# Three-pass products summed in one PSUM bank, with the difference product scaled in place

## The chip, the cores and the metric

The kernel runs on one core of a Trainium2 chip. The metric is the device time of one execution in microseconds, as the median of several runs. A separate profiled execution gives the instruction trace from which all durations below are read. TensorE (PE) does the matrix products, VectorE (DVE), ScalarE (ACT) and GpSimd (POOL) work element by element, and SyncE (SP) issues most transfers.

## The reference

Two blocks follow each other. The first is a polynomial attention over 4 batches, 4 heads, 1088 tokens and a head size of 32: queries and keys are sketched to 64 features, and attention is linear in them. Its output becomes a matrix x of 4352 tokens by 128 columns. The second block is a gated feed-forward layer, and the change lies in it:

```python
g = x @ w_gate                      # 4352x128 @ 128x1536
silu = g * (1.0 / (1.0 + np.exp(-g)))
val = x @ w_val                     # 128x1536
return (silu * val @ w_out)         # 1536x128
```

## The kernel before

**Layout.** Everything is kept transposed: xT has 128 columns of x on the partitions and tokens along the free axis. The tokens are cut into blocks, three small ones of batch 0 first (`HEAD`), and then seven from batch 1 on, six of 480 tokens and a last one of 384 (`line`). The 1536 hidden columns are cut into 12 chunks of 128. A **unit** is one block with one chunk: a gate product g, a value product, Silu of g, and their product, which is the hidden piece hj in one of the `slots`. A **down** product multiplies a hidden piece with its chunk of w_out and sums 12 of them in one PSUM bank; `store` transposes the sum and sends it out. Where line[3:6] meets the chunks in `FINE`, the down product is itself made in three passes from a cut hidden piece (`cut_hidden`: ScalarE cuts, GpSimd takes the rest, VectorE makes the difference).

**Three-pass products.** TensorE makes a plain float32 product in two slow passes. In the loop that the change touches, most products are made instead from rounded pieces in a faster number format (called cut products below). A matrix w is cut into a high part w1, and a rest w0 which is scaled up to wb = BETA * w0; x is cut into x1 and x0; wd and xd are differences, wd = w1 - wb and xd = x1 - BETA * x0, with BETA = 4096. Then

w x = (1 + 1/BETA) * (w1 x1 + wb x0) - (1/BETA) * wd xd,

apart from rounding. That takes three passes in place of two that each last about twice as long.

**The loop.** The loop at L1353 goes through 84 units y = 0 to 83 (`END`), each with `i, j = line[y // 12], y % 12`. For y below 20 (`GATES`) the value product alone has three passes, and the gate product is plain (L977); from 20 on both have three (`both`). One unit (`cut_unit`, L966) is: the difference products wd xd (L975) into one bank or a pair; ScalarE scales them by -1/BETA into an SBUF buffer `sums` (L979); TensorE makes w1 x1 and wb x0 in another bank or pair (L985, L986); VectorE scales that by 1 + 1/BETA and adds `sums` (L987); ScalarE takes Silu (L993); GpSimd multiplies Silu with the value sum into hj (L998). With both, the last two are put off to the next unit (`ending`, `finish`). The very last unit, y = 83, is a plain one of two float32 products (`unit`, L1361, L1022).

After each unit come the down products of units that lie five or more back (L1366), and pieces of other work that are woven in: steps of the attention of later batches (`parts_of`, `group`), cutting of tokens (`cut_tokens`), of gate weights (`gate_rows`) and of down weights (`down_steps`). The lists `before` and `behind` hold work of cut hidden pieces that is due at a given unit.

**PSUM.** PS is eight banks of 512 float32 columns. `used` notes when each was last handed out, `held` those that may not be. `bank` gives the one that was used longest ago (from the loop on), `pair` the pair out of (0,1), (4,5), (6,7) that was, `wide` a named pair ("a" is 4,5 and "b" is 6,7). Bank 3 ("acc") is kept for down sums, bank 2 ("g2") too from unit 20 on. The handing out only chooses; what makes engines wait is the scheduler's tracking of who still reads or writes a bank.

**Groups.** At y = 4, 6, 20, 22 and 40 a group of TensorE work of the attention is put ahead of the unit: key sums and key sketches (y = 4), query sketches (6), numerators of batch 2 and key sums of batch 3 (20), query sketches (22), numerators of batch 3 (40). `numerators` (L767) makes small products into two pairs of banks, alternating between both pairs (L777), and then ScalarE copies the first pair to xT and VectorE the second (L794). `sketched` (L576) uses one pair, from which ScalarE copies.

**The end.** After the loop, 12 products of 128 columns (L1095, `straight`) with the roles of the operands exchanged make the last 128 tokens, with the rest of the down products of the last block between them; then a copy (L1384) and the last transfers (L1390).

Of the kernel before, what the change touches and what calls it, by code (L numbers as in the profile page):

```python
# [7 lines left out]
FP32 = mybir.dt.float32  # L8
# [11 lines left out]
def kernel(  # L20
# [28 lines left out]
    nc = tc.nc  # L49
# [48 lines left out]
    def touch(*which):  # L98
        for i in which:
            clock[0] += 1  # L100
            used[i] = clock[0]

    def hold(*tags):
        for t in tags:
            held.update((place[t], place[t] + 1) if t in "ab" else (place[t],))

    def release(*tags):
        for t in tags:
            banks = (place[t], place[t] + 1) if t in "ab" else (place[t],)
            held.difference_update(banks)  # L110
            touch(*banks)
# [10 lines left out]
        touch(i)  # L122
        return PS[:, i, :]

    def pair():

        i = min((i for i in (0, 4, 6) if i not in held), key=lambda i: max(used[i], used[i + 1]))
        touch(i, i + 1)
        return PS[:, i : i + 2, :]

    def wide(tag):
        i = place[tag]
# [475 lines left out]
    def attentions():  # L608

        yield from turn_keys(1)
        yield from turn_queries(1)
        hold("a")
        kp = wide("a")
        for i, c in enumerate(kpieces):
            key_products(kp[:, i, :], *c)
        ka = apool.tile([P, NC * H, R], FP32, tag="kas", name="kas")

        def sketch(ps, i):  # L620
            c0, c1 = kpieces[i]
            return ps[:, i, 0 : 64 * (c1 - c0)].rearrange("p (x t r) -> p x t r", t=2, r=R)

        for i, (c0, c1) in enumerate(kpieces):
            nc.scalar.copy(ka[:, H * c0 : H * c1, :], sketch(kp, i)[:, :, 0, :])
        phk = apool.tile([P, NC, H, R, R], FP32, tag="phk", name="phk")
        for n, (i, c0, c1) in enumerate(((0, 0, 3), (0, 3, 5), (1, 5, 7), (1, 7, 9))):
            first = H * (c0 - kpieces[i][0])
            kb = sketch(kp, i)[:, first : first + H * (c1 - c0), 1, :]
            key_features(phk, (ka[:, H * c0 : H * c1, :], kb), c0, c1)  # L630
            if n == 3:
                release("a")
            if n % 3 != 1:
                yield
        zs, sums = feature_sums(phk)
        for f in sums:
            f()
        yield from turn_keys(2)
        kvz = wide("a")
        key_values(kvz[:, 0, 0:F], phk, 0, NC)  # L640
        value_sums(kvz[:, 0, :], zs)
        kab, kcopies = sketched(wide("b"), key_products, 2, "kab2")
        fold(kvz[:, 0, :])
        spread = spread_out(1, kvz[:, 0, :])
        hold("a", "b")
        yield
        qab, copies = sketched(wide("a"), query_sketches, 3, "qab")
        run_copies(copies, 2)
        yield
        run_copies(kcopies, 2)  # L650
        release("a", "b")
        for n, _ in enumerate(query_step(1, qab)):
            if n % 2 == 1:
                yield
        yield
        yield
        numerators(1, spread)
        yield "first"

        phk = apool.tile([P, NC, H, R, R], FP32, tag="phk", name="phk")  # L660
        yield from features(phk, kab)
        zs, sums = feature_sums(phk)
        for f in sums:
            f()
        yield from turn_keys(3)
        yield from turn_queries(2)
        for b in (2, 3):
            yield "pe"
            if b == 3:
                numerators(2, spread)  # L670
            hold("a")
            kv = bank()
            kv_bank = [max(used, key=used.get)]
            release("a")
            key_values(kv[:, 0:F], phk, 0, NC)
            if b == 2:
                kab, copies = sketched(wide("a"), key_products, 2, "kab2")
                run_copies(copies, 2)
            value_sums(kv, zs)
            fold(kv)  # L680
            spread = spread_out(b, kv)
            touch(*kv_bank)
            yield
            yield "pe"
            qab, copies = sketched(wide("b"), query_sketches, 3, "qab")
            run_copies(copies, 2)
            yield
            if b == 2:
                yield from turn_queries(3)
                phk = late[:, NL - 6 :, :].rearrange("p s (n h i j) -> p (s n) h i j", h=1, i=R, j=R)  # L690
                phk = phk.rearrange("p (c h) o i j -> p c (h o) i j", h=H)
                yield from features(phk, kab)
                zs, sums = feature_sums(phk)
            yield from beside(query_step(b, qab), sums)
        yield "pe"
        numerators(3, spread)
        yield

# [65 lines left out]
            )  # L764
            yield

    def numerators(b, spread):  # L767
        kvr = spread[:].rearrange("p h (g d) -> p h g d", g=2)
        phT = turned[b]
        num = wide("a"), wide("b")  # L770
        for g in range(2):
            for s in range(H):
                for a in range(4):
# [162 lines left out]
    def cut_hidden(y, i, j):  # L936

        if not h_sets:
            x = []
            for tag in ("kld", "qld", "vld", "kT", "qT"):  # L940
                t = const.tile([P, 2, WB], F32R, tag=tag, name="h" + tag, bufs=1)
                x += [t[:, k, :] for k in range(2)]
            h_sets.extend(x[k : k + 3] for k in range(0, 9, 3))
        n = blocks[i][1]
        h_sets.append(h_sets.pop(0))
        h1, h0, hd = h_parts[i, j] = [x[:, 0:n] for x in h_sets[-1]]
        h = hidden[i, j][:, 0:n]
        add_to(behind, y + 2, lambda: nc.scalar.activation(h1, h, AF.Copy, scale=CUT))
        add_to(before, y + 3, lambda: nc.gpsimd.tensor_tensor(
            out=h0, in0=h, in1=whole(h1), op=ALU.subtract  # L950
        ))
        add_to(before, y + 4, lambda: nc.vector.scalar_tensor_tensor(
            out=hd, in0=whole(h0), scalar=-BETA, in1=whole(h1), op0=ALU.mult, op1=ALU.add
        ))

# [7 lines left out]
        room[1] += k  # L963
        return room[0][:, at : at + k, :]

    def cut_unit(i, j, both=False, y=None):  # L966

        t0, n = blocks[i]
        x1, x0, xd = (x[:, 0:n] for x in x_parts[i])
        ws = (wg, wv) if both else (wv,)  # L970
        parts = [[x[:, j % 3, :] for x in w_parts[id(w), j // 3]] for w in ws]
        ds = pair()[:, :, 0:n] if both else bank()[:, 0:n].unsqueeze(1)
        g = None if both else bank()[:, 0:n]
        for k, (_, _, wd) in enumerate(parts):
            nc.tensor.matmul(ds[:, k], wd, xd, start=True, stop=True)  # L975
        if not both:
            nc.tensor.matmul(g, wg[:, j, :], xT[:, t0 : t0 + n], start=True, stop=True)  # L977
        sums = doubles(len(ws))[:, :, 0:n]
        nc.scalar.activation(sums, ds, AF.Copy, scale=-1.0 / BETA)  # L979
        now(before, y)  # L980
        finish()
        now(behind, y)
        ps = pair()[:, :, 0:n] if both else bank()[:, 0:n].unsqueeze(1)
        for k, (w1, wb, _) in enumerate(parts):
            nc.tensor.matmul(ps[:, k], w1, x1, start=True, stop=False)  # L985
            nc.tensor.matmul(ps[:, k], wb, x0, start=False, stop=True)  # L986
        nc.vector.scalar_tensor_tensor(  # L987
            out=sums, in0=ps, scalar=1.0 + 1.0 / BETA, in1=sums, op0=ALU.mult, op1=ALU.add
        )

        def last():
            sg = fpool.tile([P, WB], FP32, tag="sg", name="sg", bufs=5)[:, 0:n]
            nc.scalar.activation(sg, sums[:, 0] if both else g, AF.Silu)  # L993
            slot_of[i, j] = slots.pop(0)
            hj = slot_of[i, j]
            hidden[i, j] = hj
            todo.append((i, j))
            nc.gpsimd.tensor_tensor(out=hj[:, 0:n], in0=sg, in1=sums[:, len(ws) - 1], op=ALU.mult)  # L998
            if (i, j) in DOWN:
                cut_hidden(y, i, j)  # L1000

        if both:
            ending.append(last)
        else:
            last()


    ending = []

    def finish():  # L1010
        while ending:
            ending.pop(0)()

    def unit(i, j, late=False, between=(None, None)):

# [334 lines left out]
    lows = [late[:, c, :].rearrange("p (c f) -> p c f", f=P) for c in range(4)]  # L1350
    gate_rows = []
    down_steps = cut_down()
    for y in range(END):  # L1353
        i, j = line[y // NCH], y % NCH
        if y in GROUPS:
            group()
        if y == GATES:
            hold("g2")
        if y == END - 1:
            finish()  # L1360
            unit(i, j)  # L1361
        else:
            cut_unit(i, j, both=y >= GATES, y=y)
        for _ in range(2):

            if len(todo) > min(5 + (todo[0] == (line[1], 0)), END - y + 1):  # L1366
# [54 lines left out]
```

## Time and profile before

| what | value |
|---|---|
| median of 3 runs | 284.03 us (283.66 to 284.04) |
| the profiled execution's own time | 283.83 us |
| its span (first to last instruction) | 282.0 us |
| TensorE clock granted | 0.999 of full |
| loop over units, from the first L975 to the last L1022 | about 92.4 to 273.6 us |
| VectorE's scale-and-add L987, 83 of them | 83.1 us busy, 1003 ns mean |
| ScalarE's scaling L979, 83 | 70.9 us busy, 854 ns mean |

In the rows of the profile, "PE" is a product and "PEld" its weight load, which runs beside the product before it. A product's row covers its way through the array too, so rows overlap: a 480-column cut product's row is 0.38 us long, though the next product starts 0.22 us after it. "out<-in" names the tiles, with 128x480 for 128 partitions and 480 columns. After the bar stand busy time, mean length of one, and the engine's idle time just before with what ended it. In the chain of waits, each piece is followed back from the last instruction to what released it; its time is that between releases, not the row's length. A granted clock of 1.0 means that TensorE was not slowed.

### The profile page before, as it was taken

The page shows a single profiled execution, that of the slowest core. Times are in us where ns is not written, and L with a number is a line of the kernel's source. Part 1 is how long each engine was busy: PE and PEld are TensorE (multiplying, and loading weights), DVE is VectorE, ACT ScalarE, POOL GpSimd, SP SyncE. Part 2 cuts the span into 40 slices and gives each one's busy share as a digit, 9 for nine tenths or more (in the row PEclk, how much of TensorE's full clock was granted, in tenths as well). Part 3 has the DMA queues.
Part 4 walks back from the last instruction along what each step waited for, and adds up shares of the span by engine and source line. Part 5 has one row for each costly group of instructions (what it writes and reads, how often), then busy time and mean ns, then how long its engine had stood idle before and what let it go on. Part 6 is the DMA issues. An engine that isn't in the chain of part 4 may idle for free.

```text
span 282.0 us, 5606 instructions
## 1 busy us (share of the span) xinstructions
PE 275.8 (98%) x2132; PEld 191.7 (68%) x2132; DVE 226.1 (80%) x327; ACT 177.2 (63%) x322; POOL 181.8 (64%) x176
## 2 busy tenths in 40 slices
PE   8899999999999999999999999999999999999994
PEld 7545565666656676555576776757787777778984
DVE  3997987976495977999668899749999999999741
ACT  3468666633401756645368787768888898887850
POOL 3314432279510797489935887759989999898660
PEclk9999999999999999999999999999999999999999
DMA  6574194222231123000100020001000200010021
GB/s 194 160 223 106 41 278 154 81 79 79 59 68 28 27 90 86 2 0 10 29 16 0 1 35 2 0 2 29 6 0 1 37 0 1 9 29 0 2 33 30
DMA packets 26139, 14.30 MB, mean 51 GB/s; under 512 B 19840, under 2 KB 24192, under 8 KB 26112
## 3 DMA queue, kind: packets, MB, share of 16 engines
q1 hardware_dynamic: 25456, 13.84, 19.3%
q8 instruction: 17, 0.28, 0.4%
q10 hardware_dynamic: 656, 0.10, 0.2%
q14 instruction: 10, 0.08, 0.1%
HBM read 11.41 MB, written 2.23 MB: 48 GB/s over the span
## 4 chain that ended last, share of the span: by engine, by line
PE 94%; DVE 2%; DMA 2%; ACT 1%; issue 0%; SPq 0%
PE PS L1067 26%; PE PS L1022 16%; PE PS L975 11%; PE PS L985 11%; PE PS L986 11%; PE PS L977 6%; PE PS L777 2%; PE PS L347 2%; PE PS L335 2%; PE PS L381 2%; DMA kld<-in_k_dram 2%; PE PS L1062 1%; PE PS L1059 1%; PE PS L1061 1%; PE PS L1095 1%; PE PS L490 1%
## 5 line engine op out<-in xcount | busy, mean ns | idle before, releaser
L998 POOL TENSOR_TENSOR hbuf<-sg,sum 128x480 f32<-128x480 f32 (+1 forms) x83 | 105.1, 1271 | 30.5 <-ACT sg L993 24.0
L987 DVE SCALAR_TENSOR_TENSOR sum<-PS,sum 128x960 f32<-128x960 f32 (+2 forms) x83 | 83.1, 1003 | 18.8 <-ACT sum L979 13.8
L979 ACT ACTIVATE sum<-PS 128x960 f32<-128x960 f32 (+2 forms) x83 | 70.9, 854 | 35.1 <-PE PS L975 34.2
L1067 PE MATMUL PS<-hbuf,wo 128*128 128x480 f32 (+3 forms) x142 | 57.5, 505 | 0.0
L975 PE MATMUL PS<-xd,gphq 128*128 128x480 f32 (+1 forms) x63 | 38.8, 616 | 0.0
L985 PE MATMUL PS<-x,w 128*128 128x480 f32 (+1 forms) x83 | 38.5, 464 | 0.0
L993 ACT ACTIVATE sg<-sum 128x480 f32<-128x480 f32 (+1 forms) x63 | 36.7, 582 | 1.6 <-DVE sum L987 1.3
L975 PE MATMUL PS<-xd,wd 128*128 128x480 f32 (+1 forms) x83 | 36.0, 433 | 0.0
L1067 PEld LDWEIGHTS PS<-hbuf,wo 128*128 128x128 f32 x142 | 26.6, 189 | 8.4 <-issue 0.9
L986 PE MATMUL PS<-x,wb 128*128 128x480 f32 (+1 forms) x83 | 31.2, 376 | 0.0
L1022 PE MATMUL PS<-xT,wg 128*128 128x384 f32 (+1 forms) x74 | 29.5, 480 | 0.0
L1022 PE MATMUL PS<-xT,wv 128*128 128x384 f32 (+1 forms) x74 | 28.8, 471 | 0.2 <-DVE wv L279 0.2
L1026 ACT ACTIVATE sg<-PS 128x384 f32<-128x384 f32 (+1 forms) x31 | 14.3, 466 | 21.4 <-PE PS L1022 19.6
L985 PE MATMUL PS<-x,graw 128*128 128x480 f32 (+1 forms) x63 | 23.5, 373 | 0.2 <-ACT xT L794 0.2
L975 PEld LDWEIGHTS PS<-xd,wd 128*128 128x128 f32 x83 | 15.7, 189 | 11.5 <-issue 10.0
L986 PE MATMUL PS<-x,graw 128*128 128x480 f32 (+1 forms) x63 | 23.3, 370 | 0.0
L1067 PE MATMUL PS<-hbuf,scaled 128*128 128x480 f32 x42 | 20.3, 564 | 0.0
L1022 PEld LDWEIGHTS PS<-xT,wv 128*128 128x128 f32 x74 | 13.8, 190 | 9.2 <-DVE hbuf L1037 0.9
L1022 PEld LDWEIGHTS PS<-xT,wg 128*128 128x128 f32 x74 | 13.3, 189 | 9.3 <-issue 1.2
L985 PEld LDWEIGHTS PS<-x,w 128*128 128x128 f32 x83 | 15.6, 188 | 5.8 <-issue 3.4
L986 PEld LDWEIGHTS PS<-x,wb 128*128 128x128 f32 x83 | 15.6, 188 | 5.7 <-issue 4.3
L977 PE MATMUL PS<-xT,wg 128*128 128x480 f32 x40 | 19.3, 564 | 0.0
(173 smaller groups left out, 466.5 us busy)
## 6 DMA issues: line engine op xcount, KB each, us to landing
kld<-in_k_dram SPq DMA_DIRECT2D x4, 544.0 KB, 4.2
vld<-in_v_dram SPq DMA_DIRECT2D x12, 144.0 KB, 4.5
qld<-in_q_dram SPq DMA_DIRECT2D x3, 544.0 KB, 3.4
raw<-in_moe_w_out_dram SPq DMA_DIRECT2D x4, 384.0 KB, 4.0
raw<-in_moe_w_gate_dram SPq DMA_DIRECT2D x3, 384.0 KB, 3.5
raw<-in_moe_w_val_dram SPq DMA_DIRECT2D x3, 384.0 KB, 3.8
out_dram<-o SPq DMA_DIRECT2D x16, 60.0 KB, 1.9
vld<-in_v_dram SPq DMA_DIRECT2D x4, 112.0 KB, 4.2
```

The lines of the kernel that those rows point to most:

```text
L335: nc.tensor.matmul(ps[32 * a : 32 * a + 32, 96 * (c - c0) : 96 * (c - c0) + 96], qT[:, 4 * c + a, :], s123[:, a : a + H, :, :].rearrange(" ...
L975: nc.tensor.matmul(ds[:, k], wd, xd, start=True, stop=True)
L977: nc.tensor.matmul(g, wg[:, j, :], xT[:, t0 : t0 + n], start=True, stop=True)
L979: nc.scalar.activation(sums, ds, AF.Copy, scale=-1.0 / BETA)
L985: nc.tensor.matmul(ps[:, k], w1, x1, start=True, stop=False)
L986: nc.tensor.matmul(ps[:, k], wb, x0, start=False, stop=True)
L987: nc.vector.scalar_tensor_tensor(out=sums, in0=ps, scalar=1.0 + 1.0 / BETA, in1=sums, op0=ALU.mult, op1=ALU.add)
L993: nc.scalar.activation(sg, sums[:, 0] if both else g, AF.Silu)
L998: nc.gpsimd.tensor_tensor(out=hj[:, 0:n], in0=sg, in1=sums[:, len(ws) - 1], op=ALU.mult)
L1022: nc.tensor.matmul(o[:, 0:n], w[:, j, :], xT[:, t0 : t0 + n], start=True, stop=True)
L1026: nc.scalar.activation(sg[:, 0:n], g[:, 0:n], AF.Silu)
L1067: nc.tensor.matmul(acc[i][:, 0:n], w, hidden[i, j][:, 0:n], **sides)
```

## The change

A unit is split into `start_unit` and `finish_unit`, and the loop starts unit y + 1 before it finishes unit y. All of a unit happens in one pair of banks, which is held from the start until the end: bank 0 of the pair is for the gate, bank 1 for the value. `start_unit` makes the difference product(s) there, and ScalarE scales them in place, by -1/(BETA * WHOLE) with WHOLE = 1 + 1/BETA. `finish_unit` lets TensorE add w1 x1 and wb x0 onto the scaled difference (`start=False`; for y below 20 a plain gate product goes into bank 0). Silu then reads PSUM, with WHOLE as its scale, and VectorE multiplies the value sum in PSUM by WHOLE and by Silu straight into hj. The buffer `sums`, VectorE's scale-and-add and GpSimd's product are gone, as are `ending` and `finish`. Every unit, the last too, is made so. `cut_hidden`'s steps are due one unit sooner. `pair` can hold the pair that it gives, and `let_go` frees it. In the loop the attention takes pairs by `pair()` in place of the named ones, and the key sums take bank 2; the numerators of batch 1, ahead of the loop, keep the named pairs.

```diff
-    def pair():
+    def pair(keep=None):
         i = min((i for i in (0, 4, 6) if i not in held), key=lambda i: max(used[i], used[i + 1]))
         touch(i, i + 1)
+        if keep is not None:
+            held.add(i)
+            kept[keep] = i
         return PS[:, i : i + 2, :]
+    kept = {}
+    def let_go(keep):
+        i = kept.pop(keep)
+        held.discard(i)
+        touch(i, i + 1)
...
-        numerators(1, spread)
+        numerators(1, spread, (wide("a"), wide("b")))
...
-            hold("a")
-            kv = bank()
-            kv_bank = [max(used, key=used.get)]
-            release("a")
+            kv = bank("g2")
...
-                kab, copies = sketched(wide("a"), key_products, 2, "kab2")
+                kab, copies = sketched(pair(), key_products, 2, "kab2")
...
-            qab, copies = sketched(wide("b"), query_sketches, 3, "qab")
+            qab, copies = sketched(pair(), query_sketches, 3, "qab")
...
-        num = wide("a"), wide("b")
+        num = num or (pair(), pair())
...
-        add_to(behind, y + 2, lambda: nc.scalar.activation(h1, h, AF.Copy, scale=CUT))
-        add_to(before, y + 3, lambda: nc.gpsimd.tensor_tensor(
+        add_to(behind, y + 1, lambda: nc.scalar.activation(h1, h, AF.Copy, scale=CUT))
+        add_to(before, y + 2, lambda: nc.gpsimd.tensor_tensor(
...
-        add_to(before, y + 4, lambda: nc.vector.scalar_tensor_tensor(
+        add_to(before, y + 3, lambda: nc.vector.scalar_tensor_tensor(
...
+    WHOLE = 1.0 + 1.0 / BETA
+    sums_of = {}
+    def start_unit(y, both=False):
+        i, j = line[y // NCH], y % NCH
+        n = blocks[i][1]
+        xd = x_parts[i][2][:, 0:n]
+        ws = (wg, wv) if both else (wv,)
+        ps = sums_of[y] = pair(y)[:, :, 0:n]
+        for w in ws:
+            nc.tensor.matmul(
+                ps[:, w is wv], w_parts[id(w), j // 3][2][:, j % 3, :], xd, start=True, stop=True
+            )
+        d = ps if both else ps[:, 1]
+        nc.scalar.activation(d, d, AF.Copy, scale=-1.0 / BETA / WHOLE)
+    def finish_unit(y, both=False):
+        i, j = line[y // NCH], y % NCH
+        t0, n = blocks[i]
+        x1, x0, _ = (x[:, 0:n] for x in x_parts[i])
+        ps = sums_of.pop(y)
+        now(before, y)
+        for w in (wg, wv):
+            if w is wg and not both:
+                nc.tensor.matmul(
+                    ps[:, 0], wg[:, j, :], xT[:, t0 : t0 + n], start=True, stop=True
+                )
+                continue
+            w1, wb = (w_parts[id(w), j // 3][k][:, j % 3, :] for k in range(2))
+            nc.tensor.matmul(ps[:, w is wv], w1, x1, start=False, stop=False, skip_group_check=True)
+            nc.tensor.matmul(ps[:, w is wv], wb, x0, start=False, stop=True, skip_group_check=True)
+        sg = fpool.tile([P, WB], FP32, tag="sg", name="sg", bufs=5)[:, 0:n]
+        nc.scalar.activation(sg, ps[:, 0], AF.Silu, scale=WHOLE if both else 1.0)
...
+        nc.vector.scalar_tensor_tensor(
+            out=hj[:, 0:n], in0=ps[:, 1], scalar=WHOLE, in1=sg, op0=ALU.mult, op1=ALU.mult
+        )
+        let_go(y)
+        now(behind, y)
+        if (i, j) in DOWN:
+            cut_hidden(y, i, j)
...
+    start_unit(0)
     for y in range(END):
...
-        if y == END - 1:
-            finish()
-            unit(i, j)
-        else:
-            cut_unit(i, j, both=y >= GATES, y=y)
+        if y + 1 < END:
+            start_unit(y + 1, y + 1 >= GATES)
+        finish_unit(y, y >= GATES)
```

More of the change, by code (lines that the diff above doesn't have):

```diff
@@ L681, in attentions @@
             spread = spread_out(b, kv)
-            touch(*kv_bank)
             yield
             yield "pe"
-            qab, copies = sketched(wide("b"), query_sketches, 3, "qab")
+            qab, copies = sketched(pair(), query_sketches, 3, "qab")
             run_copies(copies, 2)
@@ L765, in query_step, with numerators @@
             yield
-    def numerators(b, spread):
+    def numerators(b, spread, num=None):
         kvr = spread[:].rearrange("p h (g d) -> p h g d", g=2)
         phT = turned[b]
-        num = wide("a"), wide("b")
+        num = num or (pair(), pair())
         for g in range(2):
@@ L964, in doubles @@
         return room[0][:, at : at + k, :]
-    def cut_unit(i, j, both=False, y=None):
-        t0, n = blocks[i]
[L969 to L979, printed above, removed]
-        now(before, y)
-        finish()
-        now(behind, y)
[L983 to L1003, printed above, removed]
-        else:
-            last()
@@ L1008 @@
[L1008 to L1012, printed above, removed]
+    WHOLE = 1.0 + 1.0 / BETA
[12 more added lines that the diff above has]
+        nc.scalar.activation(d, d, AF.Copy, scale=-1.0 / BETA / WHOLE)
@@ new lines, in finish_unit @@
+    def finish_unit(y, both=False):
+        i, j = line[y // NCH], y % NCH
+        t0, n = blocks[i]
+        x1, x0, _ = (x[:, 0:n] for x in x_parts[i])
+        ps = sums_of.pop(y)
+        now(before, y)
+        for w in (wg, wv):
[9 more added lines that the diff above has]
+        nc.scalar.activation(sg, ps[:, 0], AF.Silu, scale=WHOLE if both else 1.0)
+        slot_of[i, j] = slots.pop(0)
+        hj = slot_of[i, j]
+        hidden[i, j] = hj
+        todo.append((i, j))
+        nc.vector.scalar_tensor_tensor(
+            out=hj[:, 0:n], in0=ps[:, 1], scalar=WHOLE, in1=sg, op0=ALU.mult, op1=ALU.mult
+        )
+        let_go(y)
+        now(behind, y)
+        if (i, j) in DOWN:
+            cut_hidden(y, i, j)
@@ L1352 @@
     down_steps = cut_down()
+    start_unit(0)
     for y in range(END):
-        i, j = line[y // NCH], y % NCH
         if y in GROUPS:
@@ L1358 @@
             hold("g2")
-        if y == END - 1:
-            finish()
-            unit(i, j)
-        else:
-            cut_unit(i, j, both=y >= GATES, y=y)
+        if y + 1 < END:
+            start_unit(y + 1, y + 1 >= GATES)
+        finish_unit(y, y >= GATES)
         for _ in range(2):
```

## The prediction

> **What bounds the kernel now.** I read the page's busy times and chain first, then the chain of waits in single stretches, then the timeline of a few units.
>
> ```profile
> span 282.0 us, 5606 instructions
> ...
> PE 275.8 (98%) x2132; PEld 191.7 (68%) x2132; DVE 226.1 (80%) x327; ACT 177.2 (63%) x322; POOL 181.8 (64%) x176
> ...
> PE 94%; DVE 2%; DMA 2%; ACT 1%; issue 0%; SPq 0%
> ...
> L998 POOL TENSOR_TENSOR hbuf<-sg,sum 128x480 f32<-128x480 f32 (+1 forms) x83 | 105.1, 1271 | 30.5 <-ACT sg L993 24.0
> ```
>
> TensorE is busy for 98% and is 94% of the chain that ended last. The costly POOL row, which the change removes, is not in that chain. Busy time flatters TensorE, so I look at when one product follows another. This is the chain of waits from 180 to 190 us (start, length, what):
>
> ```profile
> 183.98 0.22 PE PS L986
> 184.20 0.81 PE PS L1067 x2
> 185.01 0.60 PE PS L777 x4
> 185.61 0.03 issue
> 185.64 1.53 PE PS L777 x38
> 187.17 0.02 issue
> 187.19 0.71 ACT xT L794 x2
> 187.90 0.04 issue
> 187.95 0.48 PE PS L985
> 188.43 0.22 PE PS L986
> ```
>
> A 480-column cut product costs TensorE 0.217 us (0.22 here), a plain float32 one 0.80 (two passes, 0.81 here). The stretch also holds the one place late in the loop where TensorE visibly waits for another engine: the numerators of the last batch (L777) wait in their middle for a PSUM pair, and then L985 waits for ScalarE's copies (L794), which read the pair that it wants. Adding up, over the loop from 92 us on, what lies between one product's end and the next beyond these prices gives about 2.5 us, most of it short switches at groups. So no more than about 2.5 us can be won there. Last, three rows of the timeline for the other engines (start, us):
>
> ```profile
> 206.79 0.97 ACT L979 ACTIVATE sum<-PS 128x960 f32<-128x960 f32 x1
> ...
> 207.66 0.60 ACT L993 ACTIVATE sg<-sum 128x480 f32<-128x480 f32 x1
> ...
> 207.80 1.16 DVE L987 SCALAR_TENSOR_TENSOR sum<-PS,sum 128x960 f32<-128x960 f32 x1 [0.17 <-ACT sum L979]
> ```
>
> ScalarE's next instruction starts 0.87 us after the 0.97 us scaling began: overlapped, a scaling holds the engine for 0.87 and a Silu for about 0.5.
>
> **What the Trainium skill says.** "PSUM — Partial Sum Buffer", section "The four PSUM rules": other engines' writes neither set nor clear the bits that make a product accumulate, so a product without the starting flag adds onto ScalarE's data wherever an earlier product wrote. The change thus does what it says. Nothing in the trace of before shows adding onto such data, but L986 adds onto L985's at the same 0.217. "ScalarE: Activation LUTs", "Step-by-step: what each stage is for": PSUM is the lower-latency destination for ScalarE. No row of before has ScalarE writing PSUM. "SBUF — State Buffer", "SBUF: two separate sides": VectorE and GpSimd lock a shared port pair, and one blocks the other. The trace agrees: the gate cut of L866 takes 0.55 us with POOL idle and 1.56 with POOL at work in it for 1.15.
>
> **The change, part by part.**
>
> *POOL's product goes.* 83 x 1.271 = 105 us, all beside TensorE: worth 0 on the path. VectorE multiplies from PSUM instead: 84 x 0.645 (the L987 row of 480 columns) = 54 us, against L987's 83.1. So VectorE gets lighter and, without POOL at the shared ports, its SBUF work quicker. Neither is on the path: 0.
>
> *Scaling in place.* The same columns on ScalarE. I take L979's 0.97 for PSUM as destination; bounds: somewhat less (the skill's direction, gaining nothing off the path), or up to a third more. What matters is the new wait: the first adding product (w1 on x1) waits for ScalarE, where before only VectorE waited. Queued behind it on TensorE is everything. But the unit is begun one ahead. After the second difference product of y+1, TensorE has four products of y (0.87), a down product (0.80, or 0.65 in three passes) and the two difference products of y+2 (0.43): 1.95 to 2.10 us. ScalarE starts 0.25 us after the stream's end (208.64 to 208.89 in the timeline), takes 0.97, and 0.05 passes until TensorE goes on: 1.27. Margin 0.7 to 0.8. ScalarE's load over 12 units: 12 x (0.87 + 0.50) + 5 hidden cuts x 0.5 + 1.0 = 19.9 us against TensorE's 24.5, so a backlog clears; a unit with a hidden cut and a token cut lags by some 0.35. Cost 0. If that cover were gone, each 0.1 us missed would cost 8 us over 84 units.
>
> *Pairs of banks.* Every unit holds a pair from its start until VectorE's product has read it, and three pairs are all there are. The next user waits for Silu and product: 0.25 + 0.60 + 0.04 + 0.65 + 0.05 = 1.59 us after the unit's last stream (1.56 where Silu takes 0.57). A pair is wanted again by start y+3 of its unit y, that is, after a down, 0.43, 0.87 and a down: 2.6 to 2.9 us, 3.06 in the first 20 units (0.80 + 0.22 + 1.24 + 0.80). Margin over 1 us; VectorE's longest other instruction, the hidden cut L952 at 1.65, eats at most most of it. In the first four units there is no down product: 0.22 + 1.24 = 1.46 against 1.56. That is short by 0.1 for two units: +0.2 (0 to 0.8, since VectorE is packed there).
>
> *Numerators at unit 20.* They take two pairs at once. Two are free, but the second is that of unit 19, just ended. Before, nothing waited there. Now the fourth product waits until 1.56 us after unit 19's last stream; it would have come after the down (0.80), a switch (0.09) and 0.03, at 0.92: +0.64 (0.3 to 0.9). Behind it on TensorE stand the rest of the numerators and the key sums; ScalarE's and VectorE's copies wait with them. The start of unit 21 wants the pair that ScalarE copies from for 0.70 us, but 1.2 us of key sums cover that.
>
> *Numerators at unit 40.* The wait in their middle stays about the same (185.64 against 184.98 before). But then the start of unit 41 follows at once and needs the first numerator pair, so it waits for all of L794's 0.71 us. Before, a free pair took two difference products (0.43) during that wait. They were done earlier now, for unit 40, so they no longer fill it: +0.43 (0.3 to 0.6).
>
> *The last unit.* Before: two float32 products of 384 columns, 4 x 0.322 = 1.29 us. After: six cut products at 0.175 = 1.05: -0.24. Its other parts move: the last down product comes four 128-column products sooner, so the output's stores leave SP's and ACT's queues before the last block's own. Before, the copy L1384 ended at 278.78 and those issued at 278.99 and 279.06, behind the others: -0.2 (0 to -0.3). The last hidden piece needs 1.4 us after its streams; three down and four straight products (2.18) cover it.
>
> *The shifts of cut_hidden by one* keep the same distance to the down product, since the list of hidden pieces also fills one unit sooner: 0. No DMA is added.
>
> Sum: +0.64 + 0.43 + 0.2 - 0.24 - 0.2 = +0.83 on the profiled execution's 283.83 (span 282.0 and 1.8 around it), giving 284.66. The median of the runs lies 0.20 above it, so 284.8 on the median's scale.
>
> **Rivals.**
>
> *ScalarE becomes the pace* (slower still). If scaling in place costs a third more, or small instructions bunch, the 0.7 us margin is missed in units with hidden cuts (15) and with the down weights' cuts (about 8). At 0.1 us each, 23 x 0.1 = 2.3 us more: 287.1. For it: ScalarE is already 17 of 20 us busy from 200 us on. Against: overlapped it needs only 19.9 of 24.5.
>
> *The pairs never bind* (not slower). If the pair is back sooner at both numerators, the tail's -0.44 is all that stays: 283.83 - 0.44 + 0.20 = 283.6, within no change. It decides when Silu and product end within 0.92 us of the stream; the rows give 1.56, so only a different pair could do it. For it: VectorE is lighter.
>
> *Products come closer together* (faster). A cut product takes 0.217 us for 480 columns, a float32 pass 0.402. If the cut product could stream at just twice the pass's rate, it would take 0.201; then 0.016 is lost in each of 500, 8 us in all. If traffic on PSUM caused it, halving VectorE's reads could give back a quarter: 284.8 - 2 = 282.8. It decides below a spacing of about 0.214. Against: in the first 20 units, with half that traffic, the spacing is 0.218 too.
>
> **How the numbers follow.** My forecast, 284.2 to 285.5, has 0.55; ScalarE's pace 0.20; pairs that never bind 0.15; closer products 0.10. A measurement of this kernel can tell about 0.2% (0.57 us) from no change, so 283.46 to 284.60 counts as none. Of the forecast 0.37 is slower and 0.18 within; of the second 0.18 and 0.02; of the third 0.10 is within and 0.05 faster; the fourth is faster. Slower 0.55, same 0.30, faster 0.15. The range 283.4 to 286.6 leaves out most of the closer products and the upper half of ScalarE's pace.
>
> **What would show it.** Right: POOL's busy time down by about 100 us and VectorE's by 30 or more; the product spacing still 0.217; in the chain, ScalarE's Silu and VectorE's product ahead of L783's middle at about 139 us, and about 1 us of waiting on L800's copies before unit 41; the last unit's products 1.05 us. Wrong: adding products that wait for ScalarE unit after unit (the second case), no wait at the numerators (the third), or a spacing under 0.215 (the fourth).

## The result and the profile after

The changed kernel takes 284.74 us (median of 9 runs, 284.33 to 284.98), the kernel before in the same series 283.85 (9 runs, 283.66 to 284.05). The ratio is 1.0026, with a 95% interval of 1.0016 to 1.0037: a little slower. The profiled execution took 284.74 us itself, with a span of 283.0 against 282.0.

The page after, in the order of the first fence of before: the span, the busy times, the chain's shares, then the rows of VectorE's new product (L1012) and of the scaling in place (L989).

```profile
span 283.0 us, 5508 instructions
...
PE 275.2 (97%) x2134; PEld 192.3 (68%) x2134; DVE 174.1 (62%) x327; ACT 175.2 (62%) x323; POOL 75.3 (27%) x93
...
PE 94%; DVE 2%; DMA 2%; ACT 1%; issue 0%; SPq 0%
...
L1012 DVE SCALAR_TENSOR_TENSOR hbuf<-PS,sg 128x480 f32<-128x480 f32 (+1 forms) x84 | 54.0, 642 | 74.6 <-ACT sg L1007 73.3
L989 ACT ACTIVATE PS<-PS 128x960 f32<-128x960 f32 (+2 forms) x84 | 70.3, 838 | 39.3 <-PE PS L985 38.7
```

POOL lost 106.5 us and VectorE 52.0. That is the size of the change, and none of it shows in the time: TensorE is 94% of the chain, as before. The chain of waits around unit 40 (start, length, what) holds what was lost there:

```profile
185.82 0.80 PE PS L1073 x2
186.63 2.06 PE PS L783 x39
188.69 0.02 issue
188.71 0.71 ACT xT L800 x2
189.42 0.04 issue
189.46 0.70 PE PS L985 x2
190.16 0.22 PE PS L1004
190.37 0.22 PE PS L1005
```

L783 is the numerators' line now (L777 before). Its 2.06 us hold a wait in the middle, as the 2.16 before did (0.60 + 0.03 + 1.53). Then the difference products L985 of unit 41 wait for L800, the copies that empty the numerators' first pair. Before, two difference products were done within that wait, and the first product after it, of 0.48, was already one that adds; now both difference products come after it, in 0.70, and unit 40's adding products follow. In three rows of the timeline (start, us), ScalarE scales in place, takes Silu from PSUM, and VectorE multiplies:

```profile
206.55 0.95 ACT L989 ACTIVATE PS<-PS 128x960 f32<-128x960 f32 x1
...
207.42 0.56 ACT L1007 ACTIVATE sg<-PS 128x480 f32<-128x480 f32 x1
...
208.02 0.66 DVE L1012 SCALAR_TENSOR_TENSOR hbuf<-PS,sg 128x480 f32<-128x480 f32 x1 [1.29 <-ACT sg L1007]
```

The scaling holds ScalarE for 0.87 us, from 206.55 to 207.42, which is exactly what it held before.

**Where the microsecond came from.** I took the same landmarks in both traces: the first difference product, the numerators, the first down product after unit 40, TensorE's end, the last copy, the end of the span. Work that only stands elsewhere now (one start, 0.43; one down product, 0.81) is taken out. What is left, in us of span:

| stretch | predicted | measured |
|---|---|---|
| ahead of the loop (same program) | 0 | +0.24 |
| units 0 to 3 | +0.2 | +0.01 |
| up to and with the numerators at unit 20, and on to unit 40 | +0.64 | +0.14 |
| numerators at unit 40 and the start of unit 41 | +0.43 | +0.32 |
| units 41 to 82 | 0 | -0.05 |
| last unit | -0.24 | -0.25 |
| from TensorE's end to the end of the span | -0.2 | +0.62 |
| sum | +0.83 | +1.02 (rounded entries give 1.03) |

The forecast is met (its sum is 284.86 on the median's scale, which it gives as 284.8), but two of its terms were 0.7 us too high together and one was 0.8 too low. The experiments had to explain these.

**The tail.** After the last copy before, the span goes on for 3.22 us; after, for 3.84. This is the DMA view of the changed kernel from 278 us to the end: the instruction queue's packets, megabytes and share, then each group of the last transfers with its size and the median time to landing.

```profile
q14 instruction: 1, 0.01, 0.7%
...
out_dram<-o_last SPq DMA_DIRECT2D x2, 16.0 KB, 1.9
out_dram<-o_last ACTq DMA_DIRECT2D x2, 16.0 KB, 1.9
```

In the kernel before the same two groups landed in 1.5 and 1.6 us, and that window has no instruction packet. The packet is 8 KB of program, read from 280.57 to 281.17 us, just when the output's last pieces are under way. Of the 16 parts of each of the two last transfers, 15 had landed by 281.30 and 281.07; the last ones came at 282.12 and 281.95, and the end of the kernel waits for them. That it is ScalarE's is inferred from counts: of the ten such packets within the span, four come when ScalarE has 63, 191, 320 and 449 records behind it, one per 128 or so (three of the others fit VectorE's count in the same way: 192, 320 and 447). The changed kernel has 452 records on ScalarE, so the fourth falls on its last instructions; before has 440 and never gets there. That is a correlation so far.

### The profile page after: what moved, and what is told of

Its sections match the earlier page's. It is cut to its first block, busy times and chain, and to the rows that moved or that the text cites. A ratio compares the mean times of both kernels' runs of the same rounds, so it can differ in the third digit from the quotient of the medians.

```text
span 283.0 us, 5508 instructions
## 1 busy us (share of the span) xinstructions
PE 275.2 (97%) x2134; PEld 192.3 (68%) x2134; DVE 174.1 (62%) x327; ACT 175.2 (62%) x323; POOL 75.3 (27%) x93
## 4 chain that ended last, share of the span: by engine, by line
PE 94%; DVE 2%; DMA 2%; ACT 1%; issue 0%; SPq 0%
PE PS L1073 26%; PE PS L1028 15%; PE PS L985 11%; PE PS L1005 11%; PE PS L1004 11%; PE PS L999 6%; PE PS L783 2%; PE PS L357 2%; PE PS L345 2%; DMA kld<-in_k_dram 2%; PE PS L391 2%; PE PS L1068 1%; PE PS L1065 1%; PE PS L1067 1%; PE PS L1101 1%; PE PS L500 1%
## 5 line engine op out<-in xcount | busy, mean ns | idle before, releaser
L1012 DVE SCALAR_TENSOR_TENSOR hbuf<-PS,sg 128x480 f32<-128x480 f32 (+1 forms) x84 | 54.0, 642 | 74.6 <-ACT sg L1007 73.3
L989 ACT ACTIVATE PS<-PS 128x960 f32<-128x960 f32 (+2 forms) x84 | 70.3, 838 | 39.3 <-PE PS L985 38.7
L1007 ACT ACTIVATE sg<-PS 128x480 f32<-128x480 f32 (+1 forms) x84 | 46.7, 556 | 4.6 <-PE PS L999 3.7
L985 PE MATMUL PS<-xd,gphq 128*128 128x480 f32 (+1 forms) x64 | 40.3, 630 | 0.8 <-ACT xT L800 0.8
L1004 PE MATMUL PS<-x,w 128*128 128x480 f32 (+1 forms) x84 | 38.7, 461 | 0.0
L985 PE MATMUL PS<-xd,wd 128*128 128x480 f32 (+1 forms) x84 | 35.8, 428 | 0.0
L1005 PE MATMUL PS<-x,wb 128*128 128x480 f32 (+1 forms) x84 | 31.5, 375 | 0.0
L1028 PE MATMUL PS<-xT,wg 128*128 128x384 f32 (+1 forms) x72 | 28.7, 480 | 0.0
L1028 PE MATMUL PS<-xT,wv 128*128 128x384 f32 (+1 forms) x72 | 28.0, 471 | 0.2 <-DVE wv L289 0.2
L985 PEld LDWEIGHTS PS<-xd,wd 128*128 128x128 f32 x84 | 15.9, 189 | 12.3 <-issue 9.0
L1004 PE MATMUL PS<-x,graw 128*128 128x480 f32 (+1 forms) x64 | 23.9, 374 | 0.0
L1005 PE MATMUL PS<-x,graw 128*128 128x480 f32 (+1 forms) x64 | 23.7, 370 | 0.0
L1004 PEld LDWEIGHTS PS<-x,w 128*128 128x128 f32 x84 | 15.8, 188 | 6.0 <-issue 3.8
L1005 PEld LDWEIGHTS PS<-x,wb 128*128 128x128 f32 x84 | 15.8, 188 | 5.5 <-issue 4.0
L985 PEld LDWEIGHTS PS<-xd,gphq 128*128 128x128 f32 x64 | 12.0, 188 | 10.9 <-ACT PS L989 7.5
```

The costliest lines, as they stand in the source:

```text
L985: nc.tensor.matmul(ps[:, w is wv], w_parts[id(w), j // 3][2][:, j % 3, :], xd, start=True, stop=True)
L989: nc.scalar.activation(d, d, AF.Copy, scale=-1.0 / BETA / WHOLE)
L1004: nc.tensor.matmul(ps[:, w is wv], w1, x1, start=False, stop=False, skip_group_check=True)
L1005: nc.tensor.matmul(ps[:, w is wv], wb, x0, start=False, stop=True, skip_group_check=True)
L1007: nc.scalar.activation(sg, ps[:, 0], AF.Silu, scale=WHOLE if both else 1.0)
L1012: nc.vector.scalar_tensor_tensor(out=hj[:, 0:n], in0=ps[:, 1], scalar=WHOLE, in1=sg, op0=ALU.mult, op1=ALU.mult)
```

## The experiments

Eight of the ten start from the changed kernel with small ScalarE copies ahead of the loop (e1_pads), so that the tail is out of the way; e2 is the kernel before with such copies, and e10 leaves them out again. Ratios are to the kernel before, which ran in each series; they are not the quotients of the medians. e1 to e4 ran together, then e5 to e8, then e9 and e10, each series on another chip, and the kernel before had a median of 284.03, 283.88 and 283.90 in them. Between series, medians are therefore good to some 0.15 us only, and smaller differences are read from the traces. None leaves out a part of the computation.

**e1_pads and e2_before_pads: move the instruction fetch.** The changed kernel gets 16 copies of one column each in a stretch where ScalarE is idle, so that the fourth fetch comes earlier. The kernel before gets 12, which brings its own fourth fetch to the end.

```diff
     todo.sort()
+    pad = const.tile([P, 16], FP32, name="pad")
+    for c in range(16):
+        nc.scalar.copy(pad[:, c : c + 1], ident[:, c : c + 1])
```

> The changed kernel with 16 tiny copies on ScalarE in the idle time ahead of the loop, so that ScalarE's 449th instruction, at which 8 KB of its program are fetched, comes before the last transfers and not during them. Theory (the fetch holds up one sixteenth of the last two transfers by 0.8 us): the last landing follows the last copy by about 2.2 us instead of 2.9, and the time is 283.9 to 284.2. Rival (the late landing is chance, or comes from the other end of the transfer): no change, 284.7.

> The kernel before with 12 such tiny copies, so that ScalarE's program is as long as the changed kernel's and the fetch falls on its last transfers. Theory: 0.4 to 0.8 us slower than before, 284.3 to 284.6, with late landings in the trace. Rival: 283.85 as before.

Measured: e1_pads 283.46 us, ratio 0.9989 (0.9975 to 1.0004). Its fetch is at 268.13 us, with 447 of ScalarE's records behind it, and from the last copy to the end it takes 2.95 us in place of 3.84. The DMA view of e1_pads over the same last stretch shows no instruction packet, and:

```profile
out_dram<-o_last SPq DMA_DIRECT2D x2, 16.0 KB, 1.4
out_dram<-o_last ACTq DMA_DIRECT2D x2, 16.0 KB, 1.6
```

e2_before_pads 284.48, ratio 1.0014 (1.0000 to 1.0028), within the expected range. It has a fetch at 282.02 us, 1.66 after its last copy, and 3.88 us from that copy to the end in place of 3.22; its transfers land in 1.8 and 1.8. (Its profiled execution also began the loop 1.8 us late, ahead of anything that was changed; the tail is counted from its own copy.)

So the fetch costs 0.9 us at the end of the changed kernel (3.84 against 2.95) and can be given to the kernel before; in all eight changed kernels with the copies, e1 and e3 to e9, that stretch is 2.95 or 2.96. The fetch is not all that the copies move: e1's median is 1.28 us below the changed kernel's, more than the 0.5 to 0.8 expected. Besides the tail, its trace is 0.40 shorter ahead of the loop, where runs differ as much by chance, and 0.20 shorter in it; no run shows why. The pair also shows that the prediction's -0.2 was there: without a fetch the tail is 2.95 against 3.22 before, -0.27.

**e3_finish_first: take the wait for the copies away.** At unit 40, the unit is finished between the numerators and the start of unit 41.

```diff
+        if y == 40:
+            finish_unit(y, True)
         if y + 1 < END:
             start_unit(y + 1, y + 1 >= GATES)
-        finish_unit(y, y >= GATES)
+        if y != 40:
+            finish_unit(y, y >= GATES)
```

> As e1_pads, but at unit 40 the unit is finished before unit 41 is started, so that four products stand between the last batch's numerators and the product that wants the pair ScalarE copies from. Theory (0.89 us of TensorE's idle time there is that wait, 0.2 of it the switch): 0.6 to 0.7 us faster than e1_pads, about 283.3. Rival (the wait only moves, to unit 41's adding products or the next pair): equal to e1_pads.

Measured: 282.81, ratio 0.9954 (0.9941 to 0.9967), which is faster than both kernels and 0.65 us below e1_pads, as expected. From the numerators to the first down product after unit 40 it takes 3.45 us, against 4.31 in both the changed kernel and e1_pads. The chain of waits of e3_finish_first:

```profile
186.61 2.02 PE PS L783 x39
188.63 0.43 PE PS L1004
```

The adding product L1004 goes on where L985 waited, while the copies run beside it. That removes 0.86 us of this stretch, more than the +0.32 by which the changed kernel was worse there: the kernel before had part of this wait too. The wait in the numerators' middle (2.02) stays.

**e4_value_first: the wait at unit 20 as it was predicted.** For units below 20 the value products come ahead of the gate product, so that Silu has to wait for the unit's last product.

```diff
-        for w in (wg, wv):
+        for w in (wg, wv) if both else (wv, wg):
```

> As e1_pads, but in units 0 to 19 the value products come before the gate product, so that Silu has to wait for the end of the unit. Theory (Silu waits for the gate's bank alone, which gave 0.43 us that the prediction did not count): the numerators at unit 20 wait 0.4 to 0.5 us longer in their middle, and units 3 and 4 wait 0.1 to 0.2 each for a pair: 0.4 to 0.8 us slower than e1_pads. Rival (the wait at unit 20 was short for another reason, VectorE's lighter load): equal to e1_pads.

Measured: 285.11, ratio 1.0031 (1.0019 to 1.0044). That is 1.65 above e1_pads, twice what was expected at most. The rival, no difference, is out. In the changed kernel, Silu of unit 19 starts at 138.16 us, though the unit's last product is on TensorE until about 138.5. In e4_value_first it starts after the gate product, and the numerators' second pair waits for what follows. Three rows of e4's timeline, with idle time and what ended it in brackets:

```profile
139.24 0.57 ACT L1007 ACTIVATE sg<-PS 128x480 f32<-128x480 f32 x1 [0.28 <-PE PS L999]
139.84 0.66 DVE L1012 SCALAR_TENSOR_TENSOR hbuf<-PS,sg 128x480 f32<-128x480 f32 x1 [1.73 <-ACT sg L1007]
...
140.55 1.01 PEld L783 LDWEIGHTS PS<-phT,spread 32*32 32x32 f32 x58 [0.47 <-DVE hbuf L1012]
```

The numerators take 2.06 us to the key sums, 0.38 more than the 1.68 of e1_pads. The first units lose too, in two ways. In unit 0, L1004 has no gate product ahead of it and waits for ScalarE's scaling; by the chain that unit costs 0.68 more. In unit 3, the first difference product waits 0.23 for VectorE's product of unit 0, which now ends 1.30 us after the row of that unit's last product in place of 1.06. 0.38 + 0.68 + 0.23 = 1.29, and from loop start to TensorE's end e4 is 1.30 longer than e1_pads. Unit 0's wait I had not foreseen; the other two sum to 0.61, which is within what was expected.

**e5_plain_last: undo the last unit alone.**

```diff
-        if y + 1 < END:
+        if y + 1 < END - 1:
             start_unit(y + 1, y + 1 >= GATES)
-        finish_unit(y, y >= GATES)
+        if y == END - 1:
+            unit(line[y // NCH], y % NCH)
+        else:
+            finish_unit(y, y >= GATES)
```

> The changed kernel with 16 small ScalarE copies ahead of the loop (as in e1_pads), but with the last unit plain again: two float32 products of 384 columns in two free banks in place of six cut products. Theory (the last unit's part of the sum): products of 384 columns take 4 x 0.322 = 1.29 us in place of 6 x 0.175 = 1.05, so TensorE's end comes 0.24 us later than in e1_pads (counted from the down product after unit 40), and the time is 0.1 to 0.4 us above e1_pads' 283.46. Rival (the last unit is limited by what follows it, not by its products): no difference at TensorE's end, because the last products wait for the hidden piece in either case.

Measured: 283.70, 0.24 above e1_pads; ratio 0.9993 (0.9985 to 1.0001). From the down product after unit 40 to TensorE's end: 88.21 us against 87.97, +0.24. The term stands as it was worked out.

**e6_scalar_128 and e7_scalar_480: how much room ScalarE has.** One more ScalarE instruction in each unit, after Silu and product.

```diff
+        junk = fpool.tile([P, WB], FP32, tag="sg", name="junk", bufs=5)
+        nc.scalar.copy(junk[:, 0:128], xT[:, 0:128])
         let_go(y)
```

> As e1_pads, with one more ScalarE instruction in each of the 84 units, after Silu: a copy of 128 columns into a buffer that nobody reads (about 0.2 us each). Theory (ScalarE has room: by the sum 19.9 of 24.5 us in 12 units): 12 x 0.2 = 2.4 us more make 22.3 of 24.5, a backlog still clears, and the time stays within 0.8 us of e1_pads' 283.46 (units with hidden cuts and token cuts may miss by a little). Rival (ScalarE is already close to setting the pace): 84 x 0.2 = 17 us of work show up in a good part, the time rises by 2 us or more, and adding products L985 wait for ScalarE's scaling unit after unit.

> As e6_scalar_128, with a copy of 480 columns (about 0.5 us each). Theory: 19.9 + 12 x 0.5 = 25.9 us in 12 units, above TensorE's 24.5. ScalarE now sets the pace in the busy units: 1.4 us in each of seven rounds of 12 units would be 10 us if each were as busy as the busiest; with the rounds without hidden cuts (23.4 to 24.4 of 24.5) hidden, 2 to 8 us above e1_pads' 283.46. In the chain of waits, L985 follows ScalarE's scaling L989 in many units. Rival (room is far larger than the sum says): within 0.6 us of e1_pads.

Measured: e6 283.48, ratio 0.9984 (0.9977 to 0.9990), 0.02 us from e1_pads with 14.4 us more ScalarE work (191.0 against 176.6); from loop start to TensorE's end both take 186.1 us. e7 286.40, ratio 1.0083 (1.0063 to 1.0103), 2.94 above e1_pads with 35.6 us more. In a stretch of e7's chain of waits TensorE is gone:

```profile
215.07 0.49 ACT sg L1007
215.56 0.32 ACT junk L1016
215.87 1.02 ACT PS L989
216.89 0.49 ACT sg L1007
217.38 0.48 ACT junk L1016
```

One ScalarE instruction follows another, and in e7 ScalarE is busy for all 25.0 us of 213 to 238. So ScalarE's load was judged rightly: 0.2 us more for each unit still fits, 0.5 doesn't. The rival "ScalarE becomes the pace" is real, but the changed kernel is more than 0.17 us a unit (14.4 / 84) away from it.

**e8_group_between: no wait at either numerator.** At units 20 and 40 the unit is finished ahead of the group, so both pairs that the numerators take have long been free.

```diff
+        if y in (20, 40):
+            finish_unit(y, True)
         if y in GROUPS:
             group()
...
         if y + 1 < END:
             start_unit(y + 1, y + 1 >= GATES)
-        finish_unit(y, y >= GATES)
+        if y not in (20, 40):
+            finish_unit(y, y >= GATES)
```

> As e3_finish_first, but at units 20 and 40 the unit is finished ahead of the group of attention work too, and the next one is begun after it. Then both pairs that the numerators take have been free for a unit. Theory (the waits at the two numerators are all waits for a pair of banks): the wait in the middle goes at both, 0.16 us at unit 20 (1.66 against 1.50 us) and about 0.5 us at unit 40 (2.06 against 1.5 us), and the wait for the copies stays gone as in e3: 282.81 - 0.65, so 282.0 to 282.4. Rival (the waits only move: the copies of the numerators come earlier and then delay Silu or the scaling behind them on ScalarE): no more than 0.2 us below e3_finish_first, with new waits of L985 for L989 in units 21 and 41.

Measured: 281.97 us, ratio 0.9927 (0.9912 to 0.9943), the fastest of all. The chain of waits of e8_group_between at unit 40:

```profile
186.77 1.48 PE PS L783 x38
188.25 0.66 PE PS L985 x2
```

The numerators take 1.48 us there and at unit 20, and nothing waits for the copies. From loop start to TensorE's end it is 0.69 us shorter than e3_finish_first, for 0.65 expected. Of the rival's new waits, two are there, in units 21 and 41, of 0.08 us each.

**e9_product_twice: how much room the pairs have.** From unit 24 on VectorE makes the product twice, and each pair is held 0.65 us longer.

```diff
+        if y >= 24:
+            junk = fpool.tile([P, WB], FP32, tag="sg", name="junk", bufs=5)
+            nc.vector.scalar_tensor_tensor(
+                out=junk[:, 0:n], in0=ps[:, 1], scalar=WHOLE, in1=sg, op0=ALU.mult, op1=ALU.mult
+            )
```

> As e8_group_between, but from unit 24 on VectorE makes the unit's product twice, the first time into a buffer that nobody reads. That holds each pair of banks 0.65 us longer in 60 units (39 us more on VectorE, which is busy for half of that stretch). Theory (a pair comes back over 1 us ahead of its next user): the time stays within 0.5 us of e8_group_between's 281.97; the units with a hidden cut or a token cut on VectorE may lose a little. Rival (the pairs are nearly the limit in the steady state too): difference products wait for VectorE in many of the 60 units, and the time rises by 2 us or more.

Measured: 282.69, 0.72 above e8; ratio 0.9960 (0.9944 to 0.9976). The median is above the expected 0.5, and far from 2. In the trace TensorE's end comes only 0.28 later (counted from the loop's start), and 0.23 of it is at the numerators of unit 40 (1.71 us in place of 1.48), which take a pair soon after its unit. No difference product of the 60 units waits. So the pairs have over 0.65 us of room in the steady state. The profiled execution, at 282.11, is the fastest of 11 (up to 283.94). Over all executions the median span is 280.6 us, 0.45 above e8's 280.15, so within what was expected. The other 0.27 of the median lies outside the span: four of the 11 executions took 2.2 to 2.8 us more than their span, where about 1.8 is usual. Why is not known.

**e10_no_pads: the fastest version without its small copies.**

```diff
-    pad = const.tile([P, 16], FP32, name="pad")
-    for c in range(16):
-        nc.scalar.copy(pad[:, c : c + 1], ident[:, c : c + 1])
```

> As e8_group_between, without the 16 small ScalarE copies ahead of the loop. They cost 16 x 0.06, about 1 us, of ScalarE in a stretch where it is idle. Theory (the last transfers of the changed kernel land late because ScalarE's instruction fetch falls on them, and the small copies move it away): the end follows the last copy by 3.8 us again in place of about 2.95, and the time is 0.6 to 1.0 us above e8_group_between's 281.97. Rival (the tail of the changed kernel was chance, and the four runs with small copies had luck): within 0.2 us of e8_group_between.

Measured: 282.44, 0.47 above e8; ratio 0.9950 (0.9933 to 0.9968). Neither expectation. The fetch is near the end again, at 277.88 us, but this is 0.26 after the last copy, where the last transfers are only being issued; they land in 1.5 and 1.7 us, and the tail is 3.07. In the changed kernel the fetch came 1.39 after the copy, in e2_before_pads 1.66. So the fetch cost 0.6 us or more only where it fell on the transfers themselves, and I had been wrong on where it would fall here. Of the 0.62 us by which e10's span exceeds e8's, 0.11 is tail and 0.28 lies ahead of the loop. The other 0.23 is in the loop, 0.14 of it between the numerators of unit 20 and those of unit 40. That same stretch is 0.14 longer in the changed kernel than in e1_pads, and 0.16 longer in the kernel before than in e2_before_pads, so it goes with the small copies, though no run shows how. The clock is not the reason: e10's granted clock was full up to 279.8 us, and TensorE's last product ends at 277.3.

## Why the prediction came out right, point by point

The total was right and the direction too, but by luck, through errors that cancel: -0.50 at unit 20, -0.19 in the first units and -0.11 at unit 40, against +0.24 ahead of the loop and +0.82 in the tail. From loop start to TensorE's end, where the prediction had +1.03, the change cost 0.17 us (186.27 against 186.10), and 0.15 where both kernels have the small copies (186.07 in e1, 185.92 in e2). Without the fetch (0.89) and the 0.24 ahead of the loop, the span would have been 0.1 shorter than before, so what made the changed kernel slower was not what the prediction had in its sum.

- **POOL's product and VectorE's work, costed at nothing: right.** With 106 us less on POOL and 52 less on VectorE, units 41 to 82 took as long as before to 0.05 us. The Trainium skill's page "SBUF — State Buffer", section "SBUF: two separate sides", by which a VectorE instruction with two SBUF inputs and a GpSimd instruction that reads SBUF lock each other out of a shared port pair, agrees with the trace: VectorE's hidden cut, which has two such inputs, takes 0.65 us after, where POOL is idle beside it in all 15 of them, and took 1.46 to 1.67 in all but one before, where POOL was at work.

```profile
208.87 1.65 DVE L952 SCALAR_TENSOR_TENSOR hvld<-hvld,hqld 128x480 fp32r<-128x480 f32 x1
...
208.59 0.65 DVE L958 SCALAR_TENSOR_TENSOR hvld<-hvld,hqld 128x480 fp32r<-128x480 f32 x1
```

- **Scaling in place, costed at nothing: right.** On average a 128x960 scaling takes 0.96 us into PSUM against 0.97 into SBUF, in the direction that the Trainium skill gives ("ScalarE: Activation LUTs", section "Step-by-step: what each stage is for": PSUM has the lower latency). In the steady state no adding product waits for it, even with 0.17 us a unit more on ScalarE (e6). Products that add onto ScalarE's data follow each other at 0.22, so the third rival is out: with VectorE's second read of the sums gone, the spacing is still 0.217.
- **Pairs in the steady state: right** (e9). **The first four units, +0.2: wrong**, none was lost. The step that failed is the one in "Pairs of banks" that puts the free pair 1.56 us after the unit's last stream. Silu waits for the gate's bank alone, which for y below 20 is done ahead of the value products. In four rows of the timeline after, L1005 is unit 0's last product and L985 the next one on TensorE, so the stream ends at 94.52:

```profile
94.28 0.57 ACT L1007 ACTIVATE sg<-PS 128x480 f32<-128x480 f32 x1
94.30 0.38 PE L1005 MATMUL PS<-x,wb 128*128 128x480 f32 x1
...
94.52 0.38 PE L985 MATMUL PS<-xd,wd 128*128 128x480 f32 x1
...
95.12 0.62 DVE L1012 SCALAR_TENSOR_TENSOR hbuf<-PS,sg 128x480 f32<-128x480 f32 x1
```

  Silu starts 0.24 before the stream's end, where the step has 0.25 after it. VectorE's product ends 1.22 after it, within the 1.46 to the next use. With the order turned (e4) the product ends 0.24 later still, and unit 3 waits 0.23.
- **Numerators at unit 20, +0.64: mis-sized**, for the same reason. VectorE's product of unit 19 ends 1.08 us after the stream, where the step has the pair free at 1.56. The chains, before and after, give 1.50 and 1.66 us, so +0.16:

```profile
138.61 1.50 PE PS L777 x39
...
139.30 1.66 PE PS L783 x38
```

  The mechanism was right, since the wait follows Silu: it grew by 0.38 in e4, and went in e8. But the sign that was named for it, Silu and VectorE's product in the chain there, did not come, and the rival "the pairs never bind" was nearly true at this place.
- **Numerators at unit 40, +0.43: right in place, somewhat too large.** L985 waits behind L800 as said; the stretch is 0.32 longer, the middle wait being 0.1 shorter than before. (The 184.98 of that step stands in no row; before, the numerators start at 184.94 and go on at 185.64.) e3 takes the wait away and the time falls by 0.65.
- **The last unit, -0.24: right** (-0.25; e5 +0.24).
- **The tail, -0.2: wrong in sign.** The step "the output's stores leave SP's and ACT's queues before the last block's own" holds: L1390's last transfer is issued 0.44 us after the copy in e1 and was 0.73 after it before. It brings 0.27 (2.95 against 3.22). What it left out is ScalarE's instruction fetch, 0.9 us in the changed kernel.
- **Ahead of the loop, +0.24.** Both kernels run the same program there. Over all runs but e2 the loop begins between 92.08 and 92.77 us, so I take it for chance.

**What stays open**: the 0.27 us of e9's median that lie outside its span; and why the small copies go with 0.2 us less in the loop, in the changed kernel, in e8 and in the kernel before.

## What to carry to other kernels

Relieving engines that were busy but not in the chain bought nothing here; what the change moved was when buffers come free, and each new holder of a pair of banks has to be followed to the next group that wants two at once. For each such wait, ask which part of the buffer its reader really waits for: here Silu needed one bank of the pair, and the order of two products set the wait. A start one unit ahead cost nothing in the steady state, but around a group of other work the cheapest of the orders tried is to finish what is open, then do the group, then start the next: that took 1.5 us (from loop start to TensorE's end 184.61 in e8 against 186.07 in e1) and turned a loss into a gain, of 0.7% with the small copies (e8) and 0.5% without (e10).

## What the runs showed of the hardware

- By the counts above, ScalarE's program is fetched in 8 KB packets, one per some 128 of its instructions; the four in the changed kernel took 0.3 to 1.3 us. When one fell on the last transfers of the output, one of a transfer's 16 parts landed 0.5 to 0.9 us after the others, and the span ended 0.9 us later (changed kernel against e1) or 0.7 us later (e2 against before). At 0.26 us after the last copy it cost 0.1 us (e10). Adding or removing a few instructions on an engine that is nowhere near the path can thus move the end.
- An adding product onto data that ScalarE has written follows the product before it after 0.22 us, as one onto TensorE's own sums does (L1004 and L1005 in the chain after unit 40).
